# The last gate's weights between w3 and w2, and eleven chunks of w2 as wide products, in a decode block on one core

## The chip, the cores and the metric

One core of one Trainium2 chip runs the whole block; the other seven are idle. The metric is the time of one execution on the device in microseconds, the median of several runs. TensorE (PE in the profile), VectorE (DVE), ScalarE (ACT), GpSimd (POOL) and SyncE (SP) each work through a queue of their own, in order, and wait for each other by semaphores. SP issues the transfers from HBM.

## The reference

All is float32. `B` = 4 tokens (one per sequence) of width 512, attention with 32 query heads and 8 key heads over the last 2048 positions of a cache, then a gated feed-forward of width 1792.

```python
mod = (_silu(c) @ w_mod).reshape(c.shape[0], 6, 1, -1)
sa, ca, ga, sb, cb, gb = (mod[:, 0], mod[:, 1], mod[:, 2], mod[:, 3], mod[:, 4], mod[:, 5])
h = _layernorm(x, axis=-1) * (1 + ca) + sa
x = x + ga * _A_ref(h, A_k_cache, A_v_cache, A_wq, A_wo)   # attention
h = _layernorm(x, axis=-1) * (1 + cb) + sb
gate = h @ w1; up = h @ w3
x = x + gb * ((_silu(gate) * up) @ w2)
```

`gb`, the last of the six parts of `mod`, is used only in the last line.

## The kernel before, in words

The caches and weights, 101 MB, pass once through a ring of SBUF of three slots (`ring`, `slots`; a half slot is `HALF` = 8192 columns of 128 partitions). All big transfers but `wq` are issued by SP in the order of the program: `w_mod_a`, seven groups of keys and values (`kv_in`), `wo_mod`, the last group in `last_k_wo` and `last_v`, `wo`, `w1`, `w3`, and `w2` in pieces. A transfer whose place in the ring is still being read waits on SP until its readers are done, and all transfers behind it wait too. `load` issues one, in pieces where it is given cuts. A line of the trace names `ring<-w` for each of `w1`, `w3` and the pieces of `w2`.

Every instruction goes through one recorder (`Program`, so nearly all have L59 in the profile). It derives the waits from what the instructions touch; the order on each engine is the order of the code. `do.mark()` cuts the program into two parts with semaphores of their own, the first of which are cleared while the second part runs.

`wo_mod` holds half of the output projection and the four last parts of `w_mod`. `mod_columns` multiplies such a part with silu(c): 16 products, whose results lie on PE's four column groups of 32, and DVE copies them. Before, one call gives all four (`ga`, `sh`, `cb1`, `gb`), ahead of the last group of attention.

After the last group come the output projection, the residual, the norm, and the feed-forward. `ffn_in` makes 16 products with `w1` (or `w3`), has ACT and DVE copy the result out of PSUM, runs `halve` meanwhile and transposes the result on PE. `halve` brings `x1` or `gb` by two products into the layout of the output and copies it to SBUF. `hidT` is silu(gate) * up, transposed, 14 chunks of 128 rows.

The product with `w2` has two forms. Wide: one product of 512 columns for a chunk, chunk n on column group n % 4, added up in `part`; ACT copies `part` to `work`, and eight narrow products with `sames` add the four groups up in `y_ps`. Narrow (`add_rows`): eight products of 64 columns for a chunk, straight into `y_ps`. `W2_CUTS` gives the pieces in which `w2` is loaded:

```python
W2_CUTS = [0, 8, 11, 13, 14]
```

Before, chunks 0 to 7 are wide; then PE does chunks 8 to 10 narrow, the `sames` products, and chunks 11 to 13 narrow, with the mark ahead of chunk 13. DVE multiplies `y_ps` with the halved gate, adds the halved `x1`, and SP stores 32 KB.

Of the kernel before, what the change touches and what calls it, by code (L numbers as in the profile page):

```python
# [9 lines left out]
P = 128  # L10
# [2 lines left out]
NC = 4  # L13
CHUNKS = [(c, j) for c in range(4) for j in range(4 if c < 2 else 3)]
NF = len(CHUNKS)
W2_CUTS = [0, 8, 11, 13, 14]
GUESTS = 240
GUEST_AT = [(0, 0, 12), (12, 0, 12), (24, 0, 8), (64, 0, 12), (76, 0, 12), (84, 4, 12)]
EPS = 1e-5
HALF = 8192  # L20
# [124 lines left out]
                nc.sync.sem_clear(done)  # L145


def block_kernel(nc, w_mod_a, wq, guests, kv_in, wo_mod, last_k_wo, last_v, wo, w1, w3, w2, out):

# [2 lines left out]
    do = Program(nc)  # L154

    def sb(name, *shape):
        return nc.alloc_sbuf_tensor(name, (P, *shape), F32).ap()
# [4 lines left out]
    ring = sb("ring", 6 * HALF)  # L162
    slots = [ring[:, n * 2 * HALF : (n + 1) * 2 * HALF] for n in range(3)]
    s_all = nc.alloc_psum_tensor("s_ps", (P, NT * 512), F32).ap()
    s_ps = [s_all[:, t * 512 : (t + 1) * 512] for t in range(NT)]
# [4 lines left out]
    def bank():  # L170
        turn[0] += 1
        return banks[turn[0] % 2]

    def load(dst, src, cuts=(0, 1), queue="sync"):
        step = src.shape[1] // cuts[-1]
        for lo, hi in zip(cuts[:-1], cuts[1:]):
            do(queue, "dma_start", dst[:, lo * step : hi * step], src[:, lo * step : hi * step])
        return dst[:, : src.shape[1]]
# [30 lines left out]
    hidT = sb("hidT", NF, 36)  # L209
# [11 lines left out]
    sames = sb("same", 36)  # L221
# [24 lines left out]
    ss, ln, r0, ve, a, r = (sb(n, 1) for n in ("ss", "ln", "r0", "ve", "a", "r"))  # L246
# [26 lines left out]
    def mod_columns(wv, dst, n):  # L273

        pb = bank()
        for k in range(4):
            for j in range(4):
                do("tensor", "matmul", pb[32 * j : 32 * j + 32, : n * P], sc[:, k, :], wv[:, k, j, :], start=(k == 0), stop=(k == 3))
        do("vector", "tensor_copy", dst, pb[:, : n * P])
# [20 lines left out]
    hp = bank()[:44, : 6 * 32]  # L300
# [4 lines left out]
    work = sb("work", 512)  # L305
    for half in range(2):
        qp = s_ps[half]
        for k in range(4):
            for i in range(4):
                at = ((half * 4 + i) * 4 + k) * 512  # L310
                n = min(512, 16384 - GUESTS - at)
# [4 lines left out]
    for half in range(2):  # L316
# [4 lines left out]
        for i in range(R):  # L321
            src = qtp[:, i * P : (i + 1) * P].rearrange("p (g q) -> p g q", g=4)[:, :, ::8]
# [13 lines left out]
    p_sb = [p_all[:, t * 512 : (t + 1) * 512] for t in range(NT)]  # L336
# [3 lines left out]
    def heads_out(g):  # L340

        otp = bank()[:, : R * B]
        if g < G - 1:
            do("tensor", "matmul", otp, o_sum, pick, start=True, stop=True)
        else:
            for c in range(NC):
                do("tensor", "matmul", otp, work[:, c * P : (c + 1) * P], pick_c[:, c].rearrange("p r b -> p (r b)"), start=(c == 0), stop=(c == NC - 1))
        do("vector", "tensor_copy", oT[:, g].rearrange("p r b -> p (r b)"), otp)
# [41 lines left out]
    for g in range(G - 1):  # L390
# [3 lines left out]
        elif g == 4:  # L394
            wom = load(slots[0], wo_mod)
# [5 lines left out]
    w1_t = load(slots[2][:, HALF:], w1)  # L401
# [3 lines left out]

    mod_b = sb("mod_b", 512)
    ga, sh, cb1, gb = (mod_b[:, i * P : (i + 1) * P] for i in range(4))
    mod_columns(wom[:, HALF:].rearrange("p (k j i) -> p k j i", k=4, j=4), mod_b, 4)
    do("vector", "tensor_scalar_add", cb1, cb1, 1.0)
    group(G - 1, [4, 5])  # L410
    w3_t = load(slots[0][:, HALF:], w3)
    w2_t = load(slots[0][:, :HALF], w2, W2_CUTS)
    heads_out(G - 1)
    project_out(G - 2)
# [6 lines left out]
    x1, ag, tot2 = sb("x1", P), sq, sb("tot2", 1)  # L421
# [6 lines left out]
    H = P // 2  # L428
    halves = xs.rearrange("p (n c) -> p n c", n=2)

    def halve(src, dst):
        hp = o_ps[:, :H]
        for s in range(2):
            do("tensor", "matmul", hp, shifted[:, 4 - 4 * s : 4 - 4 * s + P], src[:, s * H : (s + 1) * H], start=(s == 0), stop=(s == 1))
        do("vector", "tensor_copy", dst, hp)

    def ffn_in(ws, pg, g_sb, *moved):

        ws = ws.rearrange("p (k f) -> p k f", k=4)
        for k in range(4):
            for j in range(4):
                n = min(512, FF - 512 * j)
                do("tensor", "matmul", pg[32 * j : 32 * j + 32, :n], h2T[:, k, :], ws[:, k, j * 512 : j * 512 + n], start=(k == 0), stop=(k == 3))
        do("scalar", "copy", g_sb[:96], pg[:96])
        do("vector", "tensor_copy", g_sb[96:, :256], pg[96:, :256])
        halve(*moved)
        gt = bank()
        for c in range(4):  # L450
            n, at = (128, c * 128) if c < 2 else (96, 256 + (c - 2) * 96)
            do("tensor", "transpose", gt[:, at : at + n], g_sb[:n, c * P : (c + 1) * P], ident[:n, :n])
        return gt[:, : NF * 32].rearrange("p (n i) -> p n i", i=32)[:, :, ::8]

    gate = ffn_in(w1_t, s_ps[0], p_sb[0], x1, halves[:, 0])
    eg = sb("eg", NF, B)
    do("scalar", "activation", eg, gate, AF.Exp, scale=-1.0)
    do("vector", "tensor_scalar_add", eg, eg, 1.0)
    do("vector", "reciprocal", eg, eg)
    do("vector", "tensor_mul", eg, eg, gate)  # L460
    up = ffn_in(w3_t, s_ps[1], p_sb[1], gb, halves[:, 1])
    do("vector", "tensor_mul", hidT[:, :, 4::8], eg, up)


    y_ps, y, res = s_ps[2][:, :H], p_sb[2][:, :H], p_sb[3][:, :H]

    part = s_ps[3]
    w2_t = w2_t.rearrange("p (n c) -> p n c", n=NF)
    for n in range(W2_CUTS[1]):
        i = n % 4  # L470
        do("tensor", "matmul", part[32 * i : 32 * i + 32, :], hidT[:, n, 4:], w2_t[:, n, :], start=(n < 4), stop=(n + 4 >= W2_CUTS[1]))
    do("scalar", "copy", work, part)

    def add_rows(rows, columns, start, stop):
        for s in range(2):
            for j in range(4):
                at = j * P + s * H
                do("tensor", "matmul", y_ps[32 * j : 32 * j + 32, :], rows[:, 4 - 4 * s : 36 - 4 * s], columns[:, at : at + H], start=(start and s == 0), stop=(stop and s == 1))

    for n in range(W2_CUTS[1], NF):  # L480
        if n == W2_CUTS[-2]:
            do.mark()
        if n == W2_CUTS[2]:

            add_rows(sames, work, False, False)
        add_rows(hidT[:, n], w2_t[:, n], n == W2_CUTS[1], n == NF - 1)
    do("vector", "tensor_mul", y, y_ps, halves[:, 1])
    do("vector", "tensor_add", res, y, halves[:, 0])
    do("sync", "dma_start", out, res)
# [3 lines left out]
def _layout(i):  # L493
    import numpy as np

    def a(t):
        return np.ascontiguousarray(t)

    k = i["A_k_cache"][:, :, SK - W :, :].reshape(B, G, NT, 512, DH)
    v = i["A_v_cache"][:, :, SK - W :, :].reshape(B, G, NT, NC, P, DH)  # L500
    wm = i["w_mod"].reshape(4, P, 6, 4, P)
    xc = np.concatenate([i[n].reshape(B, 4, P).transpose(2, 1, 0).reshape(P, 16) for n in ("A_x", "c")], 1)
    w2 = i["B_w2"].reshape(14, P, D)
    wq = a(i["A_wq"].reshape(4, P, G, 512).transpose(1, 2, 0, 3)).reshape(P, 16384)
    guests = np.zeros((2, 12, 6, GUESTS), np.float32)
    for n, (at, lo, hi) in enumerate(GUEST_AT):
        for m in range(2):
            guests[m, lo:hi, n] = wq[at + 32 * m + lo : at + 32 * m + hi, 16384 - GUESTS :]
    wo = a(i["A_wo"].reshape(2, 4, R, P, D).transpose(0, 3, 1, 2, 4)).reshape(2, P, 8192)
    kv = np.concatenate([k.transpose(1, 4, 2, 0, 3).reshape(G, P, 8192), v.transpose(1, 4, 2, 0, 3, 5).reshape(G, P, 8192)], 2)  # L510
    return {
        "w_mod_a": np.concatenate([a(wm[:, :, :2].transpose(1, 0, 3, 2, 4)).reshape(P, 4096), xc], 1),
        "wq": a(wq[:, : 16384 - GUESTS]),
        "guests": guests.reshape(24, 6 * GUESTS),
        "kv_in": kv[: G - 1],
        "wo_mod": np.concatenate([wo[0], a(wm[:, :, 2:].transpose(1, 0, 3, 2, 4)).reshape(P, 8192)], 1),
        "last_k_wo": np.concatenate([kv[G - 1, :, :8192], wo[1, :, :4096]], 1),
        "last_v": a(kv[G - 1, :, 8192:]),
        "wo": a(wo[1, :, 4096:]),
        "w1": a(i["B_w1"].reshape(4, P, FF).transpose(1, 0, 2)).reshape(P, 4 * FF),  # L520
        "w3": a(i["B_w3"].reshape(4, P, FF).transpose(1, 0, 2)).reshape(P, 4 * FF),
        "w2": a(np.stack([w2[4 * j + c] for c, j in CHUNKS], 1)).reshape(P, NF * D),
    }

# [14 lines left out]
```

## Time and profile before

| | us |
|---|---|
| median of 3 runs | 242.16 |
| lowest and highest | 242.08, 242.38 |
| span of the profiled execution | 240.8 |
| PE busy | 148.7 (62%) |
| DVE busy | 56.3 (23%) |
| ACT busy | 24.1 (10%) |
| chain that ended last: DMA | 60% |
| chain that ended last: PE | 31% |

The span runs from the first to the last instruction of one profiled execution. Busy shares are averages over the span. The chain is followed back from the last instruction, at each step to what released it. A fp32 product shows as two MATMUL records and two LDWEIGHTS records (PEld), so x16 stands for eight products. The time to landing of a transfer is counted from the start of its issue.

### The profile page before, as it was taken

The page shows a single profiled execution, that of the slowest core. Times are in us where ns is not written, and L with a number is a line of the kernel's source. Part 1 is how long each engine was busy: PE and PEld are TensorE (multiplying, and loading weights), DVE is VectorE, ACT ScalarE, POOL GpSimd, SP SyncE. Part 2 cuts the span into 40 slices and gives each one's busy share as a digit, 9 for nine tenths or more (in the row PEclk, how much of TensorE's full clock was granted, in tenths as well). Part 3 has the DMA queues.
Part 4 walks back from the last instruction along what each step waited for, and adds up shares of the span by engine and source line. Part 5 has one row for each costly group of instructions (what it writes and reads, how often), then busy time and mean ns, then how long its engine had stood idle before and what let it go on. Part 6 is the DMA issues. An engine that isn't in the chain of part 4 may idle for free.

```text
span 240.8 us, 2502 instructions
## 1 busy us (share of the span) xinstructions
PE 148.7 (62%) x1113; PEld 54.2 (22%) x1113; DVE 56.3 (23%) x141; ACT 24.1 (10%) x36; POOL 4.5 (2%) x12
## 2 busy tenths in 40 slices
PE   0000169982984962944867576667399719965876
PEld 0000133322322212201312222221042202422333
DVE  5000231034152024123132133130313104113210
ACT  2000000003003003001100300300200001320100
POOL 7000000000000000000000000000000000000000
PEclk9999997997696798879797799795759968995899
DMA  8999999999999999999999999999999999999994
GB/s 305 434 444 455 424 425 446 416 446 414 457 395 468 403 459 414 449 425 446 425 446 427 435 435 435 435 427 446 425 446 425 411 419 430 386 444 443 401 413 162
DMA packets 2937, 101.39 MB, mean 421 GB/s; under 512 B 472, under 2 KB 472, under 8 KB 880
## 3 DMA queue, kind: packets, MB, share of 16 engines
q1 hardware_dynamic: 2784, 92.99, 89.8%
q10 hardware_dynamic: 144, 8.27, 8.0%
q8 instruction: 8, 0.13, 0.2%
q14 instruction: 1, 0.01, 0.0%
HBM read 101.22 MB, written 0.03 MB: 420 GB/s over the span
## 4 chain that ended last, share of the span: by engine, by line
DMA 60%; PE 31%; DVE 5%; ACT 3%; issue 1%; ACTq 0%
DMA ring<-kv_in 33%; DMA ring<-w 16%; PE s_ps L59 14%; DMA ring<-w_mod_a 11%; PE bank L59 9%; PE o_ps L59 6%; DVE nm L59 3%; ACT p_sb L59 3%; PE a_ps L59 1%; DVE mod_a L59 0%; ACT work L59 0%; DVE p_sb L59 0%; DVE e L59 0%; DVE h L59 0%; DVE sq L59 0%
## 5 line engine op out<-in xcount | busy, mean ns | idle before, releaser
L59 PE MATMUL s_ps<-ring,qT 128*32 128x512 f32 x256 | 36.5, 722 | 20.3 <-DMA ring<-kv_in 13.3
L59 PE MATMUL bank<-ident,p_sb 128*128 128x128 f32 (+1 forms) x136 | 27.7, 353 | 30.8 <-ACT p_sb L59 30.7
L59 PE MATMUL o_ps<-ring,pT 128*16 128x512 f32 x256 | 38.4, 707 | 0.1
L59 PEld LDWEIGHTS bank<-ident,p_sb 128*128 128x128 f32 (+1 forms) x136 | 19.8, 178 | 52.5 <-ACT p_sb L59 31.7
L59 ACT ACTIVATE p_sb<-s_ps,nm 128x2048 f32<-128x2048 f32 (+1 forms) x11 | 16.5, 1501 | 139.7 <-DVE oT L59 104.1
L59 DVE TENSOR_REDUCE nm<-s_ps 128x1 f32<-128x2048 f32 x7 | 16.0, 2292 | 32.5 <-PE s_ps L59 32.5
L59 DVE COPY pT<-bank 128x64 f32<-128x64 f32 x32 | 7.2, 225 | 57.0 <-PE bank L59 57.0
L59 PEld LDWEIGHTS s_ps<-ring,qT 128*32 128x32 f32 x256 | 8.7, 129 | 46.9 <-issue 20.1
L59 PE MATMUL bank<-ident,xs 128*128 128x128 f32 x1 | 0.5, 476 | 27.8 <-POOL xs L59 27.8
L59 PE MATMUL s_ps<-ring,h2T 128*32 128x512 f32 (+1 forms) x64 | 9.0, 657 | 2.3 <-DMA ring<-w 2.3
L59 PE MATMUL s_ps<-ring,hT 128*32 128x512 f32 (+1 forms) x64 | 9.4, 705 | 0.0
L59 PEld LDWEIGHTS o_ps<-ring,pT 128*16 128x16 f32 x256 | 5.4, 99 | 11.9 <-issue 9.0
L59 DVE SCALAR_TENSOR_TENSOR o_own<-o_ps,rl,own 128x512 f32<-128x512 f32 x7 | 5.3, 751 | 11.1 <-PE o_ps L59 11.1
L59 PE MATMUL a_ps<-ring,oT 128*4 128x512 f32 x64 | 7.4, 592 | 0.0
L59 DVE TENSOR_REDUCE o_sum<-o_own 128x128 f32<-128x512 f32 x7 | 7.2, 1034 | 0.2
L59 PE MATMUL bank<-ring,sc 128*32 128x256 f32 (+1 forms) x64 | 6.9, 587 | 0.0
L59 PEld LDWEIGHTS bank<-ident,xs 128*128 128x128 f32 x1 | 0.2, 183 | 27.8 <-POOL xs L59 27.8
L59 DVE TENSOR_SCALAR e<-e 128x16 f32<-128x16 f32 x1 | 0.2, 175 | 23.3 <-ACT e L59 23.3
L59 DVE COPY qT<-bank 128x64 f32<-128x64 f32 x8 | 2.2, 280 | 12.4 <-PE bank L59 12.0
L59 DVE TENSOR_REDUCE mx<-s_ps 128x1 f32<-128x512 f32 x4 | 2.8, 692 | 9.0 <-PE s_ps L59 9.0
L59 PEld LDWEIGHTS s_ps<-ring,h2T 128*32 128x32 f32 x64 | 2.6, 130 | 7.3 <-issue 4.4
L59 PE MATMUL s_ps<-ring,hidT 128*32 128x64 f32 (+1 forms) x112 | 3.6, 274 | 0.3 <-DVE hidT L59 0.3
(97 smaller groups left out, 63.7 us busy)
## 6 DMA issues: line engine op xcount, KB each, us to landing
ring<-wq ACTq DMA_DIRECT2D x1, 8072.0 KB, 26.9
ring<-w SPq DMA_DIRECT2D x2, 3584.0 KB, 37.9
ring<-last_k_wo SPq DMA_DIRECT2D x1, 6144.0 KB, 30.1
ring<-last_v SPq DMA_DIRECT2D x1, 4096.0 KB, 39.5
ring<-w_mod_a SPq DMA_DIRECT2D x1, 2064.0 KB, 26.7
ring<-wo SPq DMA_DIRECT2D x1, 2048.0 KB, 41.8
ring<-w SPq DMA_DIRECT2D x1, 2048.0 KB, 43.1
ring<-w SPq DMA_DIRECT2D x1, 768.0 KB, 44.5
```

The lines of the kernel that those rows point to most:

```text
L59: op = Op(engine, lambda: getattr(getattr(self.nc, engine), method)(*args, **kw), [])
```

## The change

The sixth part of `w_mod` leaves `wo_mod` (now 14336 columns) and becomes an input of its own, `w_gate` of 2048 columns, loaded behind `w3` and ahead of `w2`, to the place in the ring of the first quarter of the last group's keys. The call of `mod_columns` ahead of the last group makes three parts; a second call makes `gb` behind the up product, where `halve` of `gb` was. `halve` of `gb` comes behind the product that makes `hidT`, with ACT for its copy. `w2` is loaded in pieces of 4, 4, 3, 2 and 1 chunks; chunks 0 to 10 are wide, then come the `sames` products, the mark, and chunks 11 to 13 narrow.

```diff
-W2_CUTS = [0, 8, 11, 13, 14]
+W2_CUTS = [0, 4, 8, 11, 13, 14]
+WIDE = 11
...
-    mod_columns(wom[:, HALF:].rearrange("p (k j i) -> p k j i", k=4, j=4), mod_b, 4)
+    mod_columns(wom[:, HALF:].rearrange("p (k j i) -> p k j i", k=4, j=4), mod_b[:, : 3 * P], 3)
     do("vector", "tensor_scalar_add", cb1, cb1, 1.0)
     group(G - 1, [4, 5])
     w3_t = load(slots[0][:, HALF:], w3)
+    wg_t = load(ring[:, 3 * HALF : 3 * HALF + 2048], w_gate)
     w2_t = load(slots[0][:, :HALF], w2, W2_CUTS)
...
-    def halve(src, dst):
+    def halve(src, dst, engine, copy):
...
-        do("vector", "tensor_copy", dst, hp)
-
-    def ffn_in(ws, pg, g_sb, *moved):
+        do(engine, copy, dst, hp)
+
+    def ffn_in(ws, pg, g_sb, meanwhile):
...
-        halve(*moved)
+        meanwhile()
...
-    gate = ffn_in(w1_t, s_ps[0], p_sb[0], x1, halves[:, 0])
+    gate = ffn_in(w1_t, s_ps[0], p_sb[0], lambda: halve(x1, halves[:, 0], "vector", "tensor_copy"))
...
-    up = ffn_in(w3_t, s_ps[1], p_sb[1], gb, halves[:, 1])
+    up = ffn_in(w3_t, s_ps[1], p_sb[1], lambda: mod_columns(wg_t.rearrange("p (k j i) -> p k j i", k=4, j=4), gb, 1))
     do("vector", "tensor_mul", hidT[:, :, 4::8], eg, up)
+    halve(gb, halves[:, 1], "scalar", "copy")
...
-    for n in range(W2_CUTS[1]):
+    for n in range(WIDE):
         i = n % 4
-        do("tensor", "matmul", part[32 * i : 32 * i + 32, :], hidT[:, n, 4:], w2_t[:, n, :], start=(n < 4), stop=(n + 4 >= W2_CUTS[1]))
+        do("tensor", "matmul", part[32 * i : 32 * i + 32, :], hidT[:, n, 4:], w2_t[:, n, :], start=(n < 4), stop=(n + 4 >= WIDE))
     do("scalar", "copy", work, part)
...
-    for n in range(W2_CUTS[1], NF):
-        if n == W2_CUTS[-2]:
-            do.mark()
-        if n == W2_CUTS[2]:
-
-            add_rows(sames, work, False, False)
-        add_rows(hidT[:, n], w2_t[:, n], n == W2_CUTS[1], n == NF - 1)
+    add_rows(sames, work, True, False)
+    do.mark()
+    for n in range(WIDE, NF):
+        add_rows(hidT[:, n], w2_t[:, n], False, n == NF - 1)
```

PE's queue at the end of the program, from the last up product on. Before (`bank<-ident,p_sb` are the transposes, `o_ps<-mod_b,ident` is `halve` of `gb`):

```order
L59 MATMUL s_ps<-ring,h2T 32x256
L59 MATMUL o_ps<-mod_b,ident 128x64 x2
L59 MATMUL bank<-ident,p_sb 128x128 x2
L59 MATMUL bank<-ident,p_sb 128x96 x2
L59 MATMUL s_ps<-ring,hidT 32x512 x8
L59 MATMUL s_ps<-ring,hidT 32x64 x24
L59 MATMUL s_ps<-work,same 32x64 x8
L59 MATMUL s_ps<-ring,hidT 32x64 x24
```

The same stretch of PE's queue now (`bank<-ring,sc` of 128 columns is the product that makes `gb`):

```order
L60 MATMUL s_ps<-ring,h2T 32x256
L60 MATMUL bank<-ring,sc 32x128 x16
L60 MATMUL bank<-ident,p_sb 128x128 x2
L60 MATMUL bank<-ident,p_sb 128x96 x2
L60 MATMUL o_ps<-mod_b,ident 128x64 x2
L60 MATMUL s_ps<-ring,hidT 32x512 x11
L60 MATMUL s_ps<-work,same 32x64 x8
L60 MATMUL s_ps<-ring,hidT 32x64 x24
```

The 24 narrow products between the wide ones and `sames` are gone, three wide ones stand in their place ahead of ACT's copy, and the product for `gb` stands ahead of the transposes.

SP's queue from the loads of `wo_mod` to the store, with its waits (a wait on `tensor` is for readers of the place in the ring). Before:

```order
L59 DMA ring<-wo_mod 128x16384 [waits part0_30_tensor]
L59 DMA ring<-last_k_wo 128x12288 [waits part0_30_tensor]
L59 DMA ring<-last_v 128x8192
L59 DMA ring<-wo 128x4096 [waits part0_30_tensor]
L59 DMA ring<-w1 128x7168 [waits part0_30_tensor]
L59 DMA ring<-w3 128x7168 [waits part0_30_tensor]
L59 DMA ring<-w2 128x4096
L59 DMA ring<-w2 128x1536
L59 DMA ring<-w2 128x1024
L59 DMA ring<-w2 128x512
```

SP's queue now:

```order
L60 DMA ring<-wo_mod 128x14336 [waits part0_31_tensor]
L60 DMA ring<-last_k_wo 128x12288 [waits part0_31_tensor]
L60 DMA ring<-last_v 128x8192
L60 DMA ring<-wo 128x4096 [waits part0_31_tensor]
L60 DMA ring<-w1 128x7168 [waits part0_31_tensor]
L60 DMA ring<-w3 128x7168 [waits part0_31_tensor]
L60 DMA ring<-w_gate 128x2048 [waits part0_31_tensor]
L60 DMA ring<-w2 128x2048 x2
L60 DMA ring<-w2 128x1536
L60 DMA ring<-w2 128x1024
L60 DMA ring<-w2 128x512
```

`w_gate` has a wait of its own, and all pieces of `w2` are issued behind it.

## Rows read from the trace of the kernel before

**Rows 1.** The page: span; DMA busy tenths and GB/s in 40 slices.

```profile
span 240.8 us, 2502 instructions
...
DMA  8999999999999999999999999999999999999994
GB/s 305 434 444 455 424 425 446 416 446 414 457 395 468 403 459 414 449 425 446 425 446 427 435 435 435 435 427 446 425 446 425 411 419 430 386 444 443 401 413 162
```

**Rows 2.** Chain that ended last, its end: start us, us, what.

```profile
190.94 38.54 DMA ring<-w
...
229.52 3.71 PE s_ps L59 x20
...
234.56 0.27 DVE hidT L59
...
234.87 2.59 PE s_ps L59 x64
...
237.49 1.31 PE s_ps L59 x64
```

**Rows 3.** SP's issues of w1, w3 and w2: start us, us, instruction.

```profile
183.61 0.33 SPq L59 DMA_DIRECT2D ring<-w  x1
...
190.94 0.33 SPq L59 DMA_DIRECT2D ring<-w  x1
...
191.31 0.91 SPq L59 DMA_DIRECT2D ring<-w  x2
...
192.26 0.91 SPq L59 DMA_DIRECT2D ring<-w  x2
```

**Rows 4.** DMA issues w1, w3, w2's pieces, store: KB each, us to landing.

```profile
ring<-w SPq DMA_DIRECT2D x1, 3584.0 KB, 37.4
...
ring<-w SPq DMA_DIRECT2D x1, 3584.0 KB, 38.5
...
ring<-w SPq DMA_DIRECT2D x1, 2048.0 KB, 43.1
ring<-w SPq DMA_DIRECT2D x1, 768.0 KB, 44.5
ring<-w SPq DMA_DIRECT2D x1, 512.0 KB, 45.3
ring<-w SPq DMA_DIRECT2D x1, 256.0 KB, 45.4
...
out<-p_sb SPq DMA_DIRECT2D x1, 32.0 KB, 1.4
```

**Rows 5.** Timeline, PE weight loads and ACT: start, us, instruction [idle before <-releaser].

```profile
235.75 0.13 PEld L59 LDWEIGHTS s_ps<-ring,hidT 128*32 128x32 f32 x4 [0.30 <-issue]
236.31 0.12 PEld L59 LDWEIGHTS s_ps<-ring,hidT 128*32 128x32 f32 x4 [0.43 <-DMA ring<-w]
236.61 0.69 PEld L59 LDWEIGHTS s_ps<-ring,hidT 128*32 128x32 f32 x44 [0.18 <-issue]
236.86 0.59 ACT L59 COPY work<-s_ps 128x512 f32<-128x512 f32 x1 [3.06 <-PE s_ps L59]
```

**Rows 6.** Timeline of PE: four parts' product, last scores, up product, halving.

```profile
187.27 3.64 PE L59 MATMUL bank<-ring,sc 128*32 128x512 f32 x32
...
197.90 5.04 PE L59 MATMUL s_ps<-ring,qT 128*32 128x512 f32 x32 [6.98 <-DMA ring<-last_k_wo]
...
229.52 3.63 PE L59 MATMUL s_ps<-ring,h2T 128*32 128x512 f32 x32 [1.69 <-DMA ring<-w]
...
233.09 0.66 PE L59 MATMUL o_ps<-mod_b,ident 128*128 128x64 f32 x4
```

**Rows 7.** Stretches: us, busy of each engine, PEclk, DMA share, GB/s.

```profile
215.00:220.00 5.00, 1.40 (x12) 0.96 (x12) 2.18 (x11) 1.05 (x3) 0.00 (x0) 0.78 1.03 442
220.00:225.00 5.00, 4.37 (x24) 1.48 (x27) 0.29 (x1) 0.00 (x0) 0.00 (x0) 0.53 1.03 442
225.00:229.50 4.50, 2.64 (x21) 1.20 (x14) 1.56 (x5) 0.80 (x2) 0.00 (x0) 1.00 0.94 401
```

More of the change, by code (lines that the diff above doesn't have):

```diff
@@ L145, in emit, with block_kernel @@
                 nc.sync.sem_clear(done)
-def block_kernel(nc, w_mod_a, wq, guests, kv_in, wo_mod, last_k_wo, last_v, wo, w1, w3, w2, out):
+def block_kernel(nc, w_mod_a, wq, guests, kv_in, wo_mod, last_k_wo, last_v, wo, w1, w3, w_gate, w2, out):
     do = Program(nc)
@@ L515, in _layout @@
         "kv_in": kv[: G - 1],
-        "wo_mod": np.concatenate([wo[0], a(wm[:, :, 2:].transpose(1, 0, 3, 2, 4)).reshape(P, 8192)], 1),
+        "wo_mod": np.concatenate([wo[0], a(wm[:, :, 2:5].transpose(1, 0, 3, 2, 4)).reshape(P, 6144)], 1),
         "last_k_wo": np.concatenate([kv[G - 1, :, :8192], wo[1, :, :4096]], 1),
@@ L521, in _layout @@
         "w3": a(i["B_w3"].reshape(4, P, FF).transpose(1, 0, 2)).reshape(P, 4 * FF),
+        "w_gate": a(wm[:, :, 5].transpose(1, 0, 2, 3)).reshape(P, 2048),
         "w2": a(np.stack([w2[4 * j + c] for c, j in CHUNKS], 1)).reshape(P, NF * D),
```

## The prediction

> **What bounds the kernel now.** I read the page's busy shares first, then the chain of work that ended last, then the queue of transfers, and last the engines in the final 12 us.
>
> The DMA row of the page stands at 9 in every slice but the first and the last, in a span of 240.8 us [rows 1]: the kernel reads its inputs as one stream, and the engines follow it. So two questions are left: does the change alter the stream, and what stands between its last pieces and the end?
>
> The chain answers the second for the kernel before [rows 2]. It leaves the DMA only once in the last 50 us: at 229.5 us, when `w3` is there. From there all is engine work: the up product, the evacuation, the product `hidT` at 234.56, the eight wide products of `w2` from 234.87, the copy of `part`, the `sames` products at 237.49. The two pieces named `s_ps` at the end are all of `w2`'s products.
>
> The landing times come from the issues and their times to landing [rows 3, 4]. The queue's rows marked x2 hold two issues 0.48 us apart (0.43 each and 0.05 between). `w1` lands at 183.61 + 37.4 = 221.0, `w3` at 190.94 + 38.5 = 229.44, `w2`'s first piece (8 chunks) at 191.31 + 43.1 = 234.41, the second (chunks 8 to 10) at 191.79 + 44.5 = 236.29, the third at 192.26 + 45.3 = 237.56, the last at 192.74 + 45.4 = 238.14. The weight load that waited for the second piece started at 236.31 [rows 5], which agrees. So `hidT` (234.82) came 0.4 us after the first piece of `w2`: before, the tail runs on `hidT`, and the second piece was there 0.3 us ahead of its turn on PE, which came at 236.61 [rows 5].
>
> How fast the stream is: `w3`'s 3584 KB took 8.43 us behind `w1`, 425 KB/us.
>
> **What the change moves, part by part.** *The gate's 1024 KB* leave `wo_mod` and come back behind `w3`. Everything between (last keys and values, `wo`, `w1`, `w3`) lands 1024/425 = 2.41 us earlier, and so does the work on it, because each step of that stretch waits for its transfer. `w2` lands where it did, since the bytes ahead of it are the same.
>
> *The issue.* `w_gate` overwrites the first quarter of the last keys, so SP holds its issue, and the five issues of `w2` behind it, until the first four score products are done: these start at 197.90 [rows 6], so about 199 before, 196.5 after. That is 5 to 7 us later than the issues of `w2` before, but the transfers ahead in the queue last until 229.44 − 2.41 = 227.0. The cover is 30 us, the cost nothing; without it `w2` itself would be late.
>
> *The gate's product.* Before, it was a quarter of 16 products of 512 columns that took 3.64 us [rows 6], so 0.9 us. There it stood ahead of the last group, in a stretch that waited for the keys at 197.90, and nothing is won by its leaving. Now it stands behind the up product, in place of the halving of the gate (0.66 us, [rows 6]), which moves behind the transposes. `hidT` comes at 234.82 − 2.41 + (0.9 − 0.66) = 232.65, if `w_gate` (229.44 plus the small addition below) is there when the up product ends at 229.52 + 3.63 − 2.41 = 230.7 [rows 6]. It is, by 1.2 us. The halving then ends at 233.3, and ACT's new small copy beside it is off the path.
>
> *The first eight chunks.* They are now wide products of pieces that land at 232.0 and 234.4 (4 chunks each). PE takes four chunks in two batches: a batch every 0.43 us (0.13 of weight loads, 0.30 between, [rows 5]). So chunks 0 to 3 end near 234.2, 4 to 7 near 235.5, and PE stands until chunks 8 to 10 land. All that the change gains for `hidT`, 2.2 us, ends in this wait: **the piece with chunks 8 to 10 is late next**.
>
> *Chunks 8 to 10* were 24 narrow products that ran from 236.61 on, while ACT copied `part` (from 236.86, [rows 5]), and the `sames` products waited for that copy, not for them. They cost the path nothing. Now they are three wide products ahead of the copy. Before, the last stretch of wide products began at 234.87 [rows 2] and held four batches; now it begins when the piece lands, 236.31 by the row, and holds two. So the copy starts 236.31 − 234.87 = 1.44 us later, less two batches of 0.43: **+0.58 us**. Three products might fill their batches better (0.215 a product, so 0.21 less) or worse (one batch more, 0.43): +0.37 to +1.01. I take 0.58, since the eight products before went in four equal batches, and three products can't be served by one.
>
> *Behind the copy* nothing changes in size: 8 `sames` products and 24 narrow ones (chunks 11 to 13), 1.31 us from 237.49 [rows 2, 5]. The third and the last piece (237.6, 238.1) are there before their turn, which comes 0.6 us later than before. Two multiplications and the store follow as before.
>
> *Two transfers more* (`w_gate`, and 8 chunks in two pieces) stand ahead of chunks 8 to 10. The price of a split: `w2`'s four transfers took 238.14 − 229.44 = 8.70 us where `w3` took 8.43 as one of the same size, so 0.27/3 = 0.09 each. From below: the last two pieces, 768 KB, took 1.85 us, 1.81 by 425 KB/us, so 0.02 each. A gain I exclude: it is the landing of the whole piece that is waited for. From above: `w3` (3584 KB in 8.43) and `w2`'s first piece (2048 KB in 4.97) leave 0.36 for each if the rest is by size. I take 0.09, as it is the same bytes in both rows: **+0.18 us** (0.04 to 0.72).
>
> The row speaks against a fixed price here. The Trainium skill ("DMA: Bandwidth & Descriptors", Anatomy of one DMA) gives each transfer about 2.0 us of fixed time, mostly the receipt of the last write. By that figure two more transfers would add 4 us; the rows above show pieces landing 0.58 us apart, so in a queue that time overlaps and the trace disagrees with adding it up.
>
> **Sum.** +0.58 + 0.18 = +0.76 us. The profiled execution has 240.8 us and the median of the runs is 242.16, so 1.36 us lie outside the span, and the change doesn't touch them: 241.56 + 1.36 = **242.92 us**.
>
> **Rivals.**
> *A, within 0.2%* (about what a measurement of this kernel can tell from no change, 0.48 us). The three products fill their batches (+0.37) and splits cost 0.02: +0.41, 242.57. For it: the last pieces' rows; against: the weight loads come by fours, and three products leave a batch unfilled.
>
> *B, the clock falls.* PE now stands twice in the last 4 us, where before it worked without a break. Before, the clock fell from 2.4 to 1.2 GHz while PE had only single products between the steps of the norm (0.78 granted in 215 to 220, 0.53 in 220 to 225), and it stayed at 1.00 in 225 to 229.5, where PE stood 1.69 us for `w3` [rows 6, 7]. After the change the two waits are 0.4 and 1.0 us long, both shorter than that one, with full groups of products around them. If the clock is at 1.2 GHz for the narrow part, that takes up to 1.31 us more: 242.92 + 1.31 = 244.2; if for the three wide products too, 0.86 more: 245.1. The Trainium skill ("TensorE: Matmul & The Clock Gate", Loop structure matters more than you think) warns of this very form, a wait for a transfer between groups of products, from which PE goes on at the low clock. The fall after 215 agrees with it, the wait ahead of 229.5 does not.
>
> *C, faster: the stream itself speeds up.* It ran at 455 GB/s (444 KB/us) in the fourth slice of the page and at 386 in the 35th [rows 1], and the change shifts what the engines do beside it. From `w1` to chunks 8 to 10 there are 3584 + 3584 + 1024 + 2048 + 768 = 11008 KB, 25.9 us at 425; at 444 they take 24.8. That is −1.11 + 0.58 = −0.53: 241.63. It decides from a stream 3% faster, 438 KB/us (0.76 us won). Against it: `w3` shows 425 and `w2`'s first piece 412 (2048 KB in 4.97 us) while the engines did different things, and a slice counts whole packets.
>
> *D, each transfer pays alone.* The store of the output, alone in its queue, took 1.4 us to land [rows 4]; two more such transfers and 0.58 give +3.4, 245.5. Against it: the four pieces of `w2`.
>
> That the change doesn't do what it says would be a late `w_gate` or a held queue; both have over 1 us of cover, above.
>
> **How the numbers follow.** The forecast has 0.65, A 0.17, B 0.09, C 0.07, D 0.02. Slower by over 0.2%: 0.65 + 0.09 + 0.02 = 0.76; within: 0.17; faster: 0.07. The range 242.4 to 243.7 takes A and the forecast with the larger parts of its bounds, and leaves out B, C and D (0.18).
>
> **What would show it.** In the profile after: the up product starts near 227.1 and `hidT` comes near 232.7; a wait of PE for a transfer of `w2` that ends near 236.5 and stands on the chain; the copy of `part` from 237.6 (before 236.86); `sames` from 238.2; the store 0.7 to 0.8 us later; granted clock 1.00 in the last 3 us. The forecast is wrong if chunks 8 to 10 land by 235.7 (C), if the three wide products take much over 0.9 us or the clock reads 0.50 (B), or if the last pieces come after their turn on PE (D).

## The result and the profile after

The changed kernel takes 242.84 us (median of 9 runs, 242.72 to 243.08), the kernel before 242.16 (9 runs beside them, 242.08 to 242.38). The ratio is 1.0027, 95% interval 1.0018 to 1.0037: slower by 0.68 us, 0.08 us from the 242.92 us of the forecast.

The page of the changed kernel, span and stream (GB/s in 40 slices), to set beside [rows 1]:

```profile
span 241.5 us, 2486 instructions
...
DMA  8999999999999999999999999999999999999993
GB/s 301 430 462 451 413 456 413 448 413 445 423 437 423 445 414 456 415 434 423 445 423 437 423 445 423 445 415 446 456 425 394 453 391 423 436 442 432 394 413 130
```

The span is 0.7 us longer and the stream as full as before. What differs is the end of the chain (start us, us, what), beside [rows 2]:

```profile
197.57 0.33 SPq L60
...
198.90 37.59 DMA ring<-w
236.49 0.04 issue
236.53 1.09 PE s_ps L60 x6
...
237.65 0.59 ACT work L60
...
238.28 1.15 PE s_ps L60 x64
```

Before, the chain left the DMA at 229.5 with `w3`. Now it leaves it at 236.49, with the piece of `w2` that holds chunks 8 to 10, and all that stands behind it are the three wide products, ACT's copy and the narrow products. The chain also runs through SP's issues (197.57 to 198.90), but only because it follows the piece back to its issue: the queue was 30 us deep there.

The timeline of the same end (start us, us, engine, instruction, [idle before it <- what ended that]), beside [rows 5, 6]:

```profile
227.52 3.21 PE L60 MATMUL s_ps<-ring,h2T 128*32 128x512 f32 x29
...
232.60 0.26 DVE L60 TENSOR_TENSOR hidT<-eg,bank 128x56 f32<-128x56 f32 x1 [0.21 <-PE bank L60]
...
233.03 1.06 PE L60 MATMUL s_ps<-ring,hidT 128*32 128x512 f32 x8
...
234.66 1.07 PE L60 MATMUL s_ps<-ring,hidT 128*32 128x512 f32 x8 [0.56 <-DMA ring<-w]
...
236.53 1.06 PE L60 MATMUL s_ps<-ring,hidT 128*32 128x512 f32 x6 [0.81 <-DMA ring<-w]
237.65 0.59 ACT L60 COPY work<-s_ps 128x512 f32<-128x512 f32 x1 [4.29 <-PE s_ps L60]
...
238.53 0.85 PE L60 MATMUL s_ps<-ring,hidT 128*32 128x64 f32 x48
...
239.97 0.35 SPq L60 DMA_DIRECT2D out<-p_sb  x1
```

`hidT` is there at 232.86, 2.0 us earlier than before. PE then stands 0.56 and 0.81 us for pieces of `w2`, and the copy of `part` starts at 237.65, 0.79 us later than before. Three wide products (x6, two records each) take 1.06 us, as long as four (x8): a batch holds one record of each product, each on its own column group, so both batches of the three have one group empty and take as long as full ones.

The issues of `w3`, `w_gate`, and the third and fifth piece of `w2` (start us, us), and times to landing (KB, us), beside [rows 3, 4]:

```profile
187.78 0.33 SPq L60 DMA_DIRECT2D ring<-w  x1
197.57 0.33 SPq L60 DMA_DIRECT2D ring<-w_gate  x1
198.90 0.43 SPq L60 DMA_DIRECT2D ring<-w  x1
199.84 4.78 SPq L60 DMA_DIRECT2D ring<-w  x1
```

```profile
ring<-w SPq DMA_DIRECT2D x1, 3584.0 KB, 39.4
ring<-w_gate SPq DMA_DIRECT2D x1, 1024.0 KB, 32.1
ring<-w SPq DMA_DIRECT2D x1, 768.0 KB, 37.6
ring<-w SPq DMA_DIRECT2D x1, 256.0 KB, 38.5
```

`w3` lands at 227.2, `w_gate` at 229.7, chunks 8 to 10 at 236.5 (236.29 before), the last piece at 238.3 (238.14 before).

### The profile page after: what moved, and what is told of

The parts are those of the page before. It is cut to its first block, busy times and chain, and to the rows that moved or that the text cites. A ratio compares the mean times of both kernels' runs of the same rounds, so it can differ in the third digit from the quotient of the medians.

```text
span 241.5 us, 2486 instructions
## 1 busy us (share of the span) xinstructions
PE 151.1 (63%) x1103; PEld 54.3 (22%) x1103; DVE 56.3 (23%) x141; ACT 24.3 (10%) x37; POOL 4.5 (2%) x12
## 4 chain that ended last, share of the span: by engine, by line
DMA 71%; PE 21%; DVE 4%; ACT 2%; issue 1%; SPq 0%; ACTq 0%
DMA ring<-kv_in 33%; DMA ring<-w 16%; DMA ring<-last_k_wo 12%; PE s_ps L60 11%; DMA ring<-w_mod_a 11%; PE bank L60 6%; PE o_ps L60 4%; DVE nm L60 2%; ACT p_sb L60 2%; ACT work L60 0%; SPq L60 0%; DVE mod_a L60 0%; DVE p_sb L60 0%; DVE e L60 0%; DVE h L60 0%
## 5 line engine op out<-in xcount | busy, mean ns | idle before, releaser
L60 PE MATMUL o_ps<-ring,pT 128*16 128x512 f32 x256 | 39.1, 717 | 0.0
L60 PE MATMUL s_ps<-ring,h2T 128*32 128x512 f32 (+1 forms) x64 | 10.1, 718 | 0.4 <-DVE h2T L60 0.4
L60 PE MATMUL bank<-ring,sc 128*32 128x256 f32 (+2 forms) x96 | 7.9, 465 | 0.0
L60 PEld LDWEIGHTS bank<-ring,sc 128*32 128x32 f32 x96 | 3.3, 128 | 3.2 <-issue 3.1
```

The source lines that it names most:

```text
L60: op = Op(engine, lambda: getattr(getattr(self.nc, engine), method)(*args, **kw), [])
```

## The experiments

The theory to test: three wide products ahead of the copy cost 0.58 us, each transfer more ahead of the end some 0.09, and the early `hidT` is worth nothing. The rival: the moved gate and its transfers cost it all, or the early `hidT` does gain and something else takes it back.

**Chunks 8 to 10 narrow again**, all else as changed:

```diff
-WIDE = 11
+WIDE = 8
```

> The changed kernel with one thing undone: chunks 8 to 10 are narrow again, behind the `sames` products. Theory (the three wide products ahead of ACT's copy cost 0.58 us, the transfers little): the copy of `part` starts near 235.9, `sames` near 236.5, the tail then waits only for the last piece of `w2` (238.3), and the last multiplication starts near 238.9 as before: 242.2 us, between 242.1 and 242.4. Rival (the moved gate and the two transfers more cost it all, the form of chunks 8 to 10 nothing): 242.8 us, as the changed kernel.

Measured: 242.47 us, ratio to the kernel before 1.0014 (1.0005 to 1.0022). The form of the three chunks is worth 0.37 us of the 0.68, and the rival of equal time falls. But 0.29 us over the kernel before are left, and they are the gate's and the transfers', which the theory had at little. The time is 0.07 us over the upper end that the theory gave. The timeline shows what ends last:

```profile
235.86 0.58 ACT L60 COPY work<-s_ps 128x512 f32<-128x512 f32 x1 [2.74 <-PE s_ps L60]
236.50 0.27 PEld L60 LDWEIGHTS s_ps<-work,same 128*32 128x32 f32 x16 [1.61 <-ACT work L60]
...
237.86 1.06 PE L60 MATMUL s_ps<-ring,hidT 128*32 128x64 f32 x48 [0.26 <-DMA ring<-w]
```

The copy and `sames` come at the expected times, 1 us earlier than in the kernel before, and nothing is won by it: PE waits until 237.86 for chunks 11 and 12, and the 48 records of the last three chunks take 1.06 us, with a wait for chunk 13 among them (it lands at 238.4), where they take 0.85 when everything has landed. The stream sets this end.

**The wide form alone**, in the kernel before:

```diff
+WIDE = 11
...
-    for n in range(W2_CUTS[1]):
+    for n in range(WIDE):
...
-    for n in range(W2_CUTS[1], NF):
+    add_rows(sames, work, True, False)
+    for n in range(WIDE, NF):
         if n == W2_CUTS[-2]:
             do.mark()
-        if n == W2_CUTS[2]:
-
-            add_rows(sames, work, False, False)
-        add_rows(hidT[:, n], w2_t[:, n], n == W2_CUTS[1], n == NF - 1)
+        add_rows(hidT[:, n], w2_t[:, n], False, n == NF - 1)
```

> The kernel before with one part of the change alone: chunks 8 to 10 are wide, ahead of the copy of `part`; the gate's weights and the pieces of `w2` are as before. Theory: `hidT` stays at 234.8, eleven wide products take six batches of 0.43 us, the copy starts at 237.7 instead of 236.86, and the end comes 0.70 to 0.86 us later: 242.9 to 243.0 us. If eleven products fill their batches (0.215 us each) the copy starts at 237.5: 242.7. Rival (the transfers are the cost): 242.2 us, as before.

Measured: 243.01 us, 1.0036 (1.0024 to 1.0048), +0.83 us on the 242.18 beside it, inside the theory's 0.70 to 0.86.

```profile
235.05 2.78 PE L60 MATMUL s_ps<-ring,hidT 128*32 128x512 f32 x22 [0.35 <-DVE hidT L60]
...
237.88 0.58 ACT L60 COPY work<-s_ps 128x512 f32<-128x512 f32 x1 [3.90 <-PE s_ps L60]
...
238.77 0.85 PE L60 MATMUL s_ps<-ring,hidT 128*32 128x64 f32 x48
```

From the first wide product to the copy it is 237.88 − 235.05 = 2.83 us, where four batches took 1.99: 0.84 for three products, so the time of two whole batches, not the 0.645 of filled ones. Without the early `hidT`, the form alone costs more than the whole change.

**Six transfers more**: the changed kernel with the first eight chunks in eight pieces.

```diff
-W2_CUTS = [0, 4, 8, 11, 13, 14]
+W2_CUTS = [0, 1, 2, 3, 4, 5, 6, 7, 8, 11, 13, 14]
```

> The changed kernel with the first eight chunks of `w2` in eight transfers instead of two: six transfers more ahead of chunks 8 to 10. Theory with 0.09 us for each transfer: their landing is 0.54 us later, 243.4 us. With the lower bound of 0.02 each: 242.96 us. If the trace of the changed kernel is right that a piece cut in two lands in the same time (4.95 us against 4.97): 242.84, no change. If each transfer paid as much as the lone store (1.4 us): over 250 us.

Measured: 243.27 us, 1.0047 (1.0035 to 1.0059), +0.43 on the changed kernel, 0.07 for each transfer. Chunks 8 to 10 land half a microsecond later, and the end follows:

```profile
237.03 1.06 PE L60 MATMUL s_ps<-ring,hidT 128*32 128x512 f32 x6 [0.81 <-DMA ring<-w]
```

(236.53 in the changed kernel.) The price is near the 0.09 that I took, far from the 0.36 above it and from that of a lone transfer.

**Seven transfers more in the kernel before**, to see whether its end had any slack against the stream:

```diff
-W2_CUTS = [0, 8, 11, 13, 14]
+W2_CUTS = [0, 1, 2, 3, 4, 5, 6, 7, 8, 11, 13, 14]
```

> The kernel before with the first eight chunks of `w2` in eight transfers instead of one: seven transfers more, nothing else. Theory (0.08 us for each transfer, as the run with six more showed, and the tail of the kernel before already at the landing of the last piece): 7 times 0.08 later, 242.7 to 242.8 us. Rival (the kernel before has slack between the last landing and the end, since its tail runs on `hidT`): less than that by the slack; with 0.5 us of slack 242.2 us.

Measured: 242.70 us, 1.0020 (1.0012 to 1.0029), +0.50 on the 242.20 beside it, 0.07 for each again. So the kernel before had next to no slack. In the profiled executions the last piece lands 0.63 us later (238.77 against 238.14; 0.13 of it is there at `w3` already), and the store is issued 0.48 us later (239.82 against 239.34): 0.15 us do not show. The last 48 records wait for `w2` as with narrow chunks above, and take 1.01 us:

```profile
238.23 0.85 PEld L60 LDWEIGHTS s_ps<-ring,hidT 128*32 128x32 f32 x48 [0.31 <-DMA ring<-w]
238.24 1.01 PE L60 MATMUL s_ps<-ring,hidT 128*32 128x64 f32 x48
```

**The gate moved, `w2` as before** (8 chunks in one piece):

```diff
-W2_CUTS = [0, 4, 8, 11, 13, 14]
-WIDE = 11
+W2_CUTS = [0, 8, 11, 13, 14]
+WIDE = 8
```

> The gate's weights are moved as in the change, but `w2` is treated as before: eight wide chunks in one piece, chunks 8 to 13 narrow. Theory: `hidT` is early (232.7), the copy of `part` is done before chunks 8 to 10 land, and only the last piece of `w2` and its eight narrow products set the end: 242.0 to 242.2 us, since before the tail was within 0.1 to 0.2 us of that bound already. Rival (the tail on `hidT` was the cost before, and taking it away gains about the 2 us by which `hidT` is earlier): under 241.5 us. Rival (the move of the gate costs): 242.6 us or more.

Measured: 244.14 us, 1.0064 (1.0041 to 1.0087), and it scatters from 242.66 to 244.49. The theory and the rival of a gain fall. The last rival, 242.6 us or more, is met as a number; the move costs, but by way of a wait that it did not name. The timeline, and three stretches around these products (us, busy of PE, PEld, DVE, ACT, POOL, granted clock, DMA share, GB/s), show it:

```profile
234.73 3.19 PE L60 MATMUL s_ps<-ring,hidT 128*32 128x512 f32 x16 [1.93 <-DMA ring<-w]
```

```profile
234.50:238.00 3.50, 3.19 (x16) 0.63 (x16) 0.00 (x0) 0.04 (x1) 0.00 (x0) 0.61 0.79 315
...
233.00:235.00 2.00, 0.27 (x4) 0.19 (x8) 0.00 (x0) 0.04 (x1) 0.00 (x0) 1.00 0.97 392
235.50:238.50 3.00, 2.42 (x12) 0.27 (x4) 0.00 (x0) 0.54 (x1) 0.00 (x0) 0.50 0.60 236
```

PE is done early and stands 1.93 us for the first eight chunks. The granted clock falls from 1.00 to 0.50 (2.4 to 1.2 GHz) between 235.0 and 235.5, and the eight products take 3.19 us where they take 1.92 in the next run.

**The same with the wait filled**: eight products of 512 columns that nothing reads stand on PE ahead of the wide ones.

```diff
     halve(gb, halves[:, 1], "scalar", "copy")
+    for k in range(2):
+        for j in range(4):
+            do("tensor", "matmul", s_ps[0][32 * j : 32 * j + 32, :], h2T[:, k, :],
+               w1_t[:, k * 512 : (k + 1) * 512], start=(k == 0), stop=(k == 1))
```

> The kernel with the gate's weights moved and `w2` treated as before (the last run, 244.14 us), plus eight products of 512 columns that nothing reads, placed on PE in the 1.9 us in which it waited for `w2`. Theory (the clock: in the last run PE stood 1.93 us, the granted clock then fell to 0.50 and the eight wide products took 3.2 us instead of 1.9): PE no longer stands, the clock stays at 1.00, and although PE does more the time falls to 242.2 to 242.4 us, with runs close together. Rival (something else in that kernel is slow, such as the landing of `w2` in one piece): 244 us, or a little more by the added products.

Measured: 242.63 us, 1.0017 (1.0008 to 1.0026), 242.43 to 243.05. PE does more and the kernel is 1.5 us faster, and it scatters no more than the kernel before beside it (242.00 to 243.02). The clock holds:

```profile
234.74 1.92 PE L60 MATMUL s_ps<-ring,hidT 128*32 128x512 f32 x16
...
236.72 0.59 ACT L60 COPY work<-s_ps 128x512 f32<-128x512 f32 x1 [3.66 <-PE s_ps L60]
...
237.36 0.43 PE L60 MATMUL s_ps<-work,same 128*32 128x64 f32 x16 [0.69 <-ACT work L60]
```

```profile
234.50:238.00 3.50, 2.73 (x65) 1.14 (x65) 0.00 (x0) 0.59 (x1) 0.00 (x0) 1.00 0.80 320
```

It stays 0.2 us above what I expected, since I had the copy done before chunks 8 to 10 land; with `sames` ahead of them in the queue, they wait on PE until 237.4, although they land at 236.4.

**Pieces of 4, 4, 5 and 1 chunks**, gate moved, chunks 8 to 13 narrow, one transfer less than in the change:

```diff
-W2_CUTS = [0, 4, 8, 11, 13, 14]
-WIDE = 11
+W2_CUTS = [0, 4, 8, 13, 14]
+WIDE = 8
```

> The gate's weights moved as in the change, chunks 8 to 13 narrow, and `w2` in pieces of 4, 4, 5 and 1 chunks: one transfer less than the changed kernel, one more than before, and no wait of PE as long as 1.9 us. Theory (only the last landing and its eight narrow products count): last landing about 238.2, 242.2 to 242.35 us, so at best equal to the kernel before. If the early `hidT` is worth anything by itself: under 241.9 us.

Measured: 243.77 us, 1.0056 (1.0035 to 1.0076), scattered from 242.8 to 244.15. I had priced forty narrow products too low:

```profile
237.87 1.55 PE L60 MATMUL s_ps<-ring,hidT 128*32 128x64 f32 x96 [0.87 <-DMA ring<-w]
```

A third piece of five chunks leaves 48 products behind one landing, 1.55 us. In the profiled execution (243.52 us) they put the store's issue 0.66 us behind that of the kernel before (240.00 against 239.34), and the store took 2.1 us to land instead of 1.4. The granted clock stayed at 1.00 there (236 to 239.5). The runs near 244 have no profile, and what made them longer is not shown.

## Why the prediction was right, step by step

*What bounds the kernel.* Right, and nearer to the stream than I put it. I read the tail of the kernel before as running on `hidT`. It did, and it reached the last piece just as that landed: chunk 13 is there at 238.14, and its first weight load starts at 238.18, with no idle time on PE. In the runs with narrow chunks and with seven transfers more, where PE does wait for that piece, the store is issued about 1.05 us behind its landing; in the kernel before it is 1.20. So that kernel stood within 0.15 us of the stream's bound.

What the 0.15 is shows in the end of its trace (the third line is the last two product records together, the fourth the very last alone):

```profile
237.74 1.05 PE L59 MATMUL s_ps<-ring,hidT 128*32 128x64 f32 x48
...
238.18 0.27 PEld L59 LDWEIGHTS s_ps<-ring,hidT 128*32 128x32 f32 x16
...
238.38 0.40 PE L59 MATMUL s_ps<-ring,hidT 128*32 128x64 f32 x2
...
238.57 0.22 PE L59 MATMUL s_ps<-ring,hidT 128*32 128x64 f32 x1
```

The 48 records behind `sames` take 1.05 us, against 0.85 in the changed kernel. That is hardly a wait for the piece: the very last record starts 0.19 us behind the one ahead of it, where in the changed kernel the two start 0.01 us apart (239.16 and 239.17). The trace names no wait for it and no other run has it, so its cause stays open. The mark is not the reason: the run with the wide form alone has it in the old place and takes 0.85.

*The moved gate.* `w3` at 227.2 (227.0 forecast), `hidT` at 232.86 (232.65), `w_gate` 1.1 us ahead of the end of the up product (1.2). The 2.2 us promised for `hidT` came as 2.0 and went into PE's waits. But that the work between comes 2.41 us earlier like its transfers, "because each step of that stretch waits for its transfer", held only where it starts. The scores and the product with `w1` now, and that product before:

```profile
195.58 6.59 PE L60 MATMUL s_ps<-ring,qT 128*32 128x512 f32 x32 [7.87 <-DMA ring<-last_k_wo]
...
219.80 6.43 PE L60 MATMUL s_ps<-ring,h2T 128*32 128x512 f32 x32 [0.39 <-DVE h2T L60]
```

```profile
221.10 5.37 PE L59 MATMUL s_ps<-ring,h2T 128*32 128x512 f32 x32 [0.60 <-DMA ring<-w]
```

The scores start 2.3 us earlier, behind a wait of PE of 7.87 us (6.98 before), and take 6.59 us instead of 5.04 [rows 6], at a mean granted clock of 0.54 instead of 0.71. The product with `w1` now waits for `h2T`, not for `w1`; it starts 1.3 us earlier and, at 0.56 instead of 0.66, ends 0.2 us earlier. PE then comes to `w3` 0.3 us after its landing, where before it had stood 1.69 us for it, and that makes the 2.0. Two errors met here by luck: the up product came 0.4 us later than forecast, and the gate's product took no longer than the halving in its place (4.44 and 4.42 us from the start of the up product to the transposes), where I had counted 0.24 more. Neither reached the end, since `hidT` was early enough with either.

*The issue.* Held until 197.6 (196.5 forecast; the scores that hold it ran slower), with no cost, as argued.

*Chunks 8 to 10.* From their first product to the copy 237.65 − 236.53 = 1.12 us; the working gave 1.99 − 0.86 = 1.13. Right, and the run with the wide form alone confirms that three products take two whole batches.

*Two transfers more.* Chunks 8 to 10 start at 236.53 against 236.31 by the row of before, +0.22 (+0.18 forecast). The price of 0.09 is 0.07 by two runs. Two of those make 0.14; the other 0.08 us is less than the times to landing, given to 0.1 us, can place.

*Behind the copy.* This is the mis-sized term: "nothing changes in size", 1.31 us. It took 1.15. The work is the same; the 0.16 is the late last record in the trace of before, which my 1.31 had in it. So +0.58 + 0.22 − 0.16 = +0.64, and the store starts at 239.97 instead of 239.34. The median says +0.68. As each kernel has one profiled execution, whether that record is late in the others too is not known.

*The sum as a sum.* The forecast added two prices. The runs show that they don't add: the form alone costs 0.83, the gate and the pieces alone 0.29, both 0.68. The end is the later of two paths, PE behind the copy and the last landing, and moving the gate gives the first path time that the wide form then takes.

*The rivals.* A and D fell: three products took the time of two whole batches, and a transfer costs 0.07 us. B, the clock, did not come about at the end of the changed kernel: the waits were 0.56 and 0.81 us, and the granted clock reads 1.00 in both stretches (columns as above):

```profile
233.00:236.00 3.00, 2.17 (x17) 0.32 (x16) 0.00 (x0) 0.21 (x1) 0.00 (x0) 1.00 0.99 398
236.00:239.50 3.50, 2.16 (x70) 1.09 (x70) 0.05 (x1) 0.59 (x1) 0.00 (x0) 1.00 0.39 156
```

But it was real: with the first eight chunks in one piece it cost 1.5 us by the medians, 1.27 of it in the eight products of the trace. I had priced it at 1.31 to 2.2. The cut in 4 and 4 is what kept the change clear of it: the run with narrow chunks differs from that one only in the cut, and has 242.47 us. The Trainium skill ("TensorE: Matmul & The Clock Gate", Loop structure matters more than you think) describes this for a long wait for a transfer between products, after which PE runs cold; the run with one piece agrees, with 3.19 us for products of 1.92 after a wait of 1.93 us. C did not come about: from the landing of `w3` to that of chunks 8 to 10 it took 236.5 − 227.2 = 9.3 us for 3840 KB, 413 KB/us.

None of the versions beats the kernel before, and the runs give the reason: with its inputs in one full stream, it ended within 0.15 us of what the last piece's landing and the products that need it allow.

## What to carry to other kernels

Where a stream of transfers sets the end, as here, work that comes earlier gains nothing; ask which piece is late next, and what stands between that landing and the store. A form of a product that is cheaper on the engine can be dearer on the path, if it stands ahead of a copy that the old form ran beside. When the end is the later of two paths, price each change on both paths, because their costs and gains don't add.

## What the runs showed of the hardware

Behind a wait of 1.93 us on PE, the granted clock fell to 0.50 (1.2 GHz), and the products took 3.19 us instead of 1.92; filling the wait with products that nobody needs was worth 1.5 us. Two of the six executions with that wait took 242.66 and 242.96 us, so it may not cost the clock each time; they have no profile. In the kernel before a wait of 1.69 us had not cost the clock [rows 6, 7].

A transfer more in a full queue costs 0.07 us, by six and by seven transfers. But SP's queue of issues is not endless: the last issue of `w2` in the changed kernel took 4.78 us instead of 0.43, with nine big transfers ahead of it that had not landed; in the kernel before, with eight ahead, it took 0.43. In the run with six transfers more the issues of five pieces went out like that, one by one (start us, us):

```profile
199.93 4.77 SPq L60 DMA_DIRECT2D ring<-w  x1
204.74 5.62 SPq L60 DMA_DIRECT2D ring<-w  x1
210.40 7.39 SPq L60 DMA_DIRECT2D ring<-w  x1
```

Chunks 8 to 10 were then issued 12.5 us ahead of their landing instead of 37.6. That was still enough, but the cover that I counted as 30 us shrinks with each piece.

In three runs (gate moved with one piece, the same filled, and 4, 4, 5, 1) the store took 1.8 to 2.1 us to land instead of 1.4 to 1.5. In each of them the trace has one more fetch of instructions than in the changed kernel (nine packets of 16 KB, not eight), within 0.7 us of the store. The run with narrow chunks has the ninth fetch too, before 239.0, half a microsecond ahead of its store, which took 1.5. That lies between the distances of the other three (0.4 to 0.7), so it speaks against the fetch as the cause, which was not tested.
